# Joined VectorE operations over one buffer, first loads in smaller pieces, and a new order of emission, in a kernel that mixes a long convolution with a token MLP

## The chip, the cores and the metric

The kernel runs on one core of a Trainium2 chip. The core has several engines, each with its own instruction stream: TensorE (matmuls, "PE" in the profile), VectorE ("DVE"), ScalarE ("ACT"), GpSimd ("POOL"), and SyncE ("SP"), which here only issues DMAs. The engines wait for each other through semaphores. The metric is the device time of one execution in microseconds; lower is better.

## The reference, cut to what matters

```python
def reference(A_q, A_k, A_v, A_shift_k, A_ssm_k, A_ssm_D, B_x, B_w1, B_b1, B_w2, B_b2, gate_w):
    def _A_ref(q, k, v, shift_k, ssm_k, ssm_D):      # S = 2048, D = 640, 4 taps
        for t in range(ks):
            k_shift = k_shift + k_pad[:, t:t + S, :] * shift_k[:, ks - 1 - t][None, None, :]
        kv = k_shift * v
        kv_f = rfft2(kv_pad);  kf_f = rfft2(kf_pad)  # both padded to 2S = 4096
        y = irfft2(kv_f * kf_f)[:, :S, :]
        y = y + kv * ssm_D[None, None, :]
        return q * y
    def _B_ref(x, w1, b1, w2, b2):                   # F = 1536
        h = _layernorm(x, axis=-1)
        u = _gelu(jnp.einsum("bsd,sf->bdf", h, w1) + b1)
        return transpose(jnp.einsum("bdf,fs->bds", u, w2) + b2)
    x = A_q
    g = _sigmoid((x * gate_w).sum(-1, keepdims=True))
    return g * _A_ref(x, ...) + (1 - g) * _B_ref(x, ...)
```

All arrays are bf16. Branch A is a convolution along the 2048 tokens, done in the frequency domain, with one filter per channel; branch B is an MLP along the tokens. A gate per token mixes the two.

## The kernel before

**Tiling.** A tile has 128 partitions. Tokens are split by their residue modulo 8, so that a "slot" holds four residues of 640 channels each: 128 x 2560 elements (`SL = 4 * D`). X (the input q, which layer normalisation overwrites in place) has four slots X0 to X3; so have k and v.

**Stages.** (1) *W stage*: the filter `ssm` is loaded in two halves, transposed on TensorE (`transp`, five blocks of 128 channels for each half), copied from PSUM to `wT` on ScalarE or VectorE, and multiplied by the cosine and sine tables `FTB` (`fwd` for odd residues, `fwd_even` for the even ones). ScalarE evicts every result from PSUM to the spectra: C0 for the first half, C1 for the second. VectorE combines them (`mixing`). `fwd` makes groups of four matmuls per eviction, `fwd_even` groups of two. (2) *kv stage*: a load of k (`kn`) is copied to another layout (`kp`, `k_turn`), transposed by a DMA into `KT` (two for each half), and multiplied by a matrix of taps `KF` that GpSimd builds; ScalarE evicts it to `ksh`, VectorE multiplies by v (`kv`). (3) *A transforms*: kv is transformed with the same tables into C2 (first half) and C3 (second half) and mixed. (4) *w1*: twelve tiles of F, each a sum of 32 products of `ring` (pieces of w1) with normalised X (four blocks of eight matmuls, one block for each X slot), gelu on ScalarE into GT. Between the tiles VectorE multiplies X by the gate weights into `gq`, and ScalarE sums the rows. (5) *Products* of the spectra on VectorE (`cross`, `product`), with some additions made by accumulating DMAs from GpSimd's queue. (6) *Inverse*: VectorE's `invmix` and TensorE's `inverse` with the tables `GTB`, twice (h = 0, 1); (7) *w2*, sixteen tiles of 24 matmuls, interleaved with the inverse; ScalarE evicts with the scale 1 - g and the bias `c2` = (1 - g) * b2 into O. The inverse's results go through `cgb` (scaled by g), are multiplied by q and added to O on VectorE. For the last tile the bias is added to `cgb` beforehand (line 573) and two last operations (line 619) take the matmul's result straight from PSUM to O.

**Buffers.** The spectra C0 to C3 and SS, and the temporary tm0 and tm1 of the products, are separate tensors, each with two or four slots; SS and tm0 follow C3 in memory. One vector operation takes one tensor as an operand, with a pattern of strides over it, so operations over slots of two tensors are separate instructions.

**Order.** The program is written as a list of operations (one entry for each vector operation, activation, DMA, or run of matmuls). `_ORDER`, at the end of the file, is the order in which they are emitted, made beforehand by a planner; each engine runs its instructions in that order. `_SLOTS` says which of the four PSUM tiles pp0 to pp3 each run of matmuls uses. A tracker looks at what each operation reads and writes and puts in the semaphore waits. So a change of the list's length changes every number in `_ORDER`. `TAKES` says which of ScalarE and VectorE does a copy of a filter tile (`wT..`), a normalisation (`ln0` to `ln15`, one for each of the 16 residue tiles of X) or a relayout of k (`kp..`). All loads are on SP's queue, in the order of emission. SP's issue of a DMA waits for the semaphores that the tracker puts ahead of it, and everything behind it on SP waits with it.

Because helpers emit the operations, the profile's lines are those of the helpers: L298 is every matmul, L559 every tensor-tensor operation (`tt`), L573 and L574 tensor-scalar operations, L603 every activation (`act`), L613 the copy of `wT` on VectorE, L619 the last two operations, L272 every plain DMA, L265 the DMA transposes, L267 the accumulating DMAs, L884 the statistics, L694 and L698 the relayout of k on VectorE and ScalarE.

```python
SSM0 = ((0, 2), (2, 5))
def tab_load(i):
    a, b = ((0, NF - 2048), (NF - 2048, NF))[i]
    dma(FTB[:, a:b], dr(ftab, a, [[NF, 128], [1, b - a]]), 256 * (b - a), tok=f"f{i}")
```

Of the kernel before, what the change touches and what calls it, by code (L numbers as in the profile page):

```python
# [440 lines left out]
def _build(nc, A_q, A_k, A_v, A_shift_k, A_ssm_k, A_ssm_D, B_x, B_w1, B_b1, B_w2, B_b2, gate_w, out):  # L441
# [10 lines left out]
    with ExitStack() as es:  # L452
# [26 lines left out]

        def base_of(h):  # L480
            return T.mem[h.name][1]

        def V(h, off, dims, p0=0, pn=128):
            row = T.mem[h.name][2]
            return bass.AP(tensor=h, offset=p0 * row + off, ap=[[row, pn]] + [list(d) for d in dims])
# [21 lines left out]
        INVE = (1,)  # L507
        FALL, GALL = len(EVEN) < 2, len(INVE) < 2
# [7 lines left out]
        C = [alloc(f"C{i}", [128, 4, 4, D], BF16) for i in range(4)]  # L516
        SS = alloc("SS", [128, 2, 4, D], BF16)
        E_base = cur[0]
# [5 lines left out]
        gq = [alloc(f"gq{i}", [128, 2, D], BF16, at=base_of(Drow) + 5120 + 2560 * i) for i in range(2)]  # L524
# [12 lines left out]
        tm = [alloc(f"tm{i}", [128, 2, 4, D], BF16, at=E_base + 2 * SL * 2 * i) for i in range(2)]  # L537
# [142 lines left out]
        def x_load(hk):  # L680
            dma(X[:, hk, :, :], row8(A_q, hk), 128 * 5120, tok=f"x{hk}", rate=400.0)
# [32 lines left out]
        SSM0 = ((0, 2), (2, 5))  # L714
        TAKES = {'wT00': 'DVE', 'wT01': 'ACT', 'wT02': 'ACT', 'wT03': 'ACT', 'wT04': 'ACT', 'ln0': 'DVE', 'ln1': 'DVE', 'ln2': 'DVE', 'ln3': 'DVE', 'ln4': 'DVE', 'ln5': 'DVE', 'ln6': 'DVE', 'ln7': 'DVE', 'ln8': 'ACT', 'ln9': 'ACT', 'ln10': 'ACT', 'ln11': 'DVE', 'ln12': 'ACT', 'ln13': 'ACT', 'ln14': 'DVE', 'ln15': 'ACT', 'kp0': 'DVE', 'kp1': 'DVE', 'wT10': 'ACT', 'wT11': 'DVE', 'wT12': 'ACT', 'wT13': 'ACT', 'wT14': 'ACT', 'kp2': 'DVE', 'kp3': 'ACT'}
        ORDER = "x0 s00 s02 x1 f0 f1 x2 x3 s10 s12 w00 w01 k0 k1 w02 w03 gw t0 t1 v0 v1 k2 k3 v2 v3 t2 t3 w10 w11 w12 w13 g w20 w21 w22 w23".split()
# [13 lines left out]
        def tab_load(i):  # L730
            a, b = ((0, NF - 2048), (NF - 2048, NF))[i]
            dma(FTB[:, a:b], dr(ftab, a, [[NF, 128], [1, b - a]]), 256 * (b - a), tok=f"f{i}")
# [11 lines left out]
        tab_load(0)  # L744
        tab_load(1)
# [144 lines left out]
        def ln_scale(a, b):  # L890
# [21 lines left out]
            o_.dur, o_.lock = 1.05, False  # L912
# [27 lines left out]
        for h in range(2):  # L940
# [8 lines left out]
            if h == 0:  # L949
# [40 lines left out]
                mixing(C[0], SS, 0, fine=True, prio=MIXP)  # L990
# [55 lines left out]
        def mixing_acc(R, Th, Ts):  # L1046
# [3 lines left out]
            def pr(h, s, rev=False):  # L1050
                return V(h, s * SL + (1280 if rev else 0), [[-1280 if rev else 1280, 2], [1, 1280]])
            for i in range(2):
                tt("DVE", sl(Th, Ts + i), sl(R, i), sl(R, 2 + i), ALU.subtract)
# [6 lines left out]
        PACC = ()  # L1060
        mixing_acc(C[2], C[1], 0) if 0 in PACC else mixing(C[2], C[1], 0)
# [8 lines left out]
        for ft in range(FT):  # L1070
# [14 lines left out]
            if ft == 0:  # L1085
                act(gq[1][:, 0, :], gwb[:, :], ACT.Copy, acc=gws[:, :], name="gws").after.add(g_)
            if ft in (1, 3, 5, 7):
                hk = ft // 2
                for a in range(2):
                    gb = gq[a]  # L1090
                    tt("DVE", gb[:, :, :], X[:, hk, 2 * a:2 * a + 2, :], V(gwb, 0, [[0, 2], [1, D]]), ALU.mult)
                    for b in range(2):
                        t = 4 * hk + 2 * a + b
                        act(gb[:, b, :], gb[:, b, :], ACT.Copy, acc=gacc[:, t:t + 1], name="gsum")
# [52 lines left out]
        npr = [0]  # L1147

# [28 lines left out]
        def half(hs, i, rev=False):  # L1177
            h, s = hs
            if rev:
                return V(h, (s + i) * SL + 1280, [[-1280, 2], [1, 1280]])  # L1180
            return V(h, (s + i) * SL, [[1280, 2], [1, 1280]])

        def comp(hs, i, c):
            h, s = hs
# [194 lines left out]
```

## Time and profile before

| what | value |
|---|---|
| time, median of 3 runs | 181.4 us (181.2, 181.4, 181.61) |
| time of the profiled execution | 181.52 us |
| its span, first to last instruction | 179.7 us |
| mean granted clock of TensorE | 0.997 |
| TensorE's last matmuls of w2 | from 172.48 us, for 3.42 us |
| last two operations on VectorE (L619) | from 175.82 us, for 1.00 us |
| vector operations of L559 on 128x2560 and on 128x5120 elements | about 1.48 us and 2.82 us each |
| eviction of a 128x640 result by ScalarE | 0.718 us each, one every 0.61 us when in a row |
| loads: SP's issue | 0.44 to 0.59 us each when the queue is free |

The span is that of the profiled execution, and all positions in the text ("at 27.56 us") count from its start. The table of landings that the prediction uses comes from the trace's record of each DMA: a load issued by SP lands when the last of the 16 DMA engines has written its part. In the views, "idle before <-releaser" says how long an engine waited and for what; a group's "x8" is a run of eight like instructions, and overlapping matmuls make the shown time of a group longer than the time to the next group's start.

| load | landed at us | load | landed at us |
|---|---|---|---|
| ssm, first half, two pieces | 4.29, 6.82 | kn (first two) | 21.11, 24.36 |
| X0 | 8.40 | X2 | 22.72 |
| FTB, first piece | 9.98 | first w1 piece | 25.73 |
| X1, X3 | 11.78, 13.35 | KT, first pair | 28.81, 31.31 |
| ssm, second half, two pieces | 15.38, 18.27 | last v piece that is ahead of the second KT pair | 46.11 |
| FTB, second piece | 19.53 | KT, second pair | 49.70, 52.66 |

### The profile page before, as it was taken

Reading aid. Unit: us, or ns where it says so; the run is one execution under the profiler, and the core shown is the slowest. Engines: PE = TensorE matmul, PEld = TensorE weight load, DVE = VectorE, ACT = ScalarE, POOL = GpSimd, SP = SyncE. Lnnn points to the kernel's source line nnn. Section 1 sums busy time; section 2 is a strip of 40 time slices with the busy share of each in tenths; the row PEclk is TensorE's granted clock in tenths of the full one; section 3 lists DMA queues with packets and bytes.
Section 4 is the critical chain, followed back from the end, with each engine's and each line's share of the span. In section 5 each row is a group of like instructions: output and inputs, shape, how many; then the busy total and the mean of one; then the engine's idle time right before and its main releaser. Section 6 shows DMA issues by size and latency. Waiting matters only on the chain.

```text
span 179.7 us, 3292 instructions
## 1 busy us (share of the span) xinstructions
PE 171.4 (95%) x1364; PEld 135.0 (75%) x1364; DVE 167.2 (93%) x195; ACT 111.4 (62%) x174; POOL 42.1 (23%) x40
## 2 busy tenths in 40 slices
PE   7998689999999999999999999999999999999991
PEld 2676436787678766767777788999999998888780
DVE  2499889989999999999999999999999999999993
ACT  3489799999999999895891231033041306555860
POOL 1059924410000305200035110220085000024300
PEclk9999999999999999999999999999999999999998
DMA  5999999999989999998968997489899998919896
GB/s 182 358 383 408 403 200 181 325 395 385 141 169 306 334 212 334 226 209 269 387 166 146 197 170 241 123 148 178 318 285 198 199 198 222 379 68 191 190 278 217
DMA packets 31659, 44.57 MB, mean 248 GB/s; under 512 B 11673, under 2 KB 21018, under 8 KB 31516
## 3 DMA queue, kind: packets, MB, share of 16 engines
q1 hardware_dynamic: 26384, 33.20, 57.4%
q0 software_dynamic: 5200, 11.14, 35.0%
q8 instruction: 11, 0.18, 0.4%
q14 instruction: 4, 0.03, 0.0%
q10 hardware_dynamic: 60, 0.01, 0.0%
HBM read 27.96 MB, written 2.62 MB: 170 GB/s over the span
## 4 chain that ended last, share of the span: by engine, by line
PE 78%; DMA 8%; DVE 5%; ACT 4%; SPq 2%; issue 1%; DVEq 0%
PE pp L298 78%; DMA FTB<-ftab 8%; ACT C L603 3%; SPq L272 2%; DVE cgb L559 2%; DVE O L559 1%; DVE C L559 1%; ACT wT L603 1%; ACT cgb L603 0%; DVE O L619 0%; DVEq L412 0%; DVE cgb L573 0%; DVE q_hi L559 0%
## 5 line engine op out<-in xcount | busy, mean ns | idle before, releaser
L559 DVE TENSOR_TENSOR C<-C 128x2560 bf16<-128x2560 bf16 (+2 forms) x41 | 58.2, 1451 | 1.1 <-ACT C L603 1.0
L298 PE MATMUL pp<-X,ring 128*128 128x320 bf16 x384 | 56.9, 299 | 0.1
L298 PE MATMUL pp<-GT,W 128*128 128x320 bf16 x384 | 54.7, 300 | 0.0
L298 PEld LDWEIGHTS pp<-GT,W 128*128 128x128 bf16 x384 | 51.9, 144 | 1.3 <-ACT O L603 0.5
L298 PEld LDWEIGHTS pp<-X,ring 128*128 128x128 bf16 x384 | 37.3, 98 | 14.6 <-issue 0.5
L603 ACT ACTIVATE C<-pp 128x640 bf16<-128x640 f32 x64 | 41.3, 718 | 3.6 <-PE pp L298 3.4
L603 ACT ACTIVATE O<-pp,c,omg 128x640 bf16<-128x640 f32 x15 | 12.9, 882 | 29.8 <-PE pp L298 29.8
L298 PE MATMUL pp<-wT,FTB 128*128 128x320 bf16 x112 | 17.6, 300 | 1.9 <-ACT wT L603 0.7
L267 POOL DMA_DIRECT2D C<-C x8 | 10.9, 1915 | 26.7 <-DVE C L559 26.7
L603 ACT ACTIVATE GT<-pp,cc 128x640 bf16<-128x640 f32 x12 | 9.6, 797 | 11.9 <-PE pp L298 11.9
L603 ACT ACTIVATE cgb<-pp,gg 128x640 bf16<-128x640 f32 x16 | 12.2, 792 | 7.2 <-PE pp L298 7.0
L298 PEld LDWEIGHTS pp<-wT,FTB 128*128 128x128 bf16 x112 | 9.8, 97 | 8.3 <-ACT C L603 3.0
L559 DVE TENSOR_TENSOR tm<-C,C 128x2560 bf16<-128x2560 bf16 (+1 forms) x7 | 14.4, 2057 | 0.0
L267 POOL DMA_DIRECT2D C<-q_hi x6 | 5.9, 984 | 35.9 <-DVE q_hi L559 20.4
L884 DVE BATCH_NORM_STATS2 stats<-X 128x6 f32<-128x320 bf16 x32 | 13.4, 474 | 0.8 <-DMA X<-in_A_q_dram 0.7
L298 PE MATMUL pp<-C,GTB 128*128 128x320 bf16 x80 | 12.5, 299 | 0.0
L603 ACT ACTIVATE gq<-gq 128x640 bf16<-128x640 bf16 x16 | 11.7, 737 | 0.0
L559 DVE TENSOR_TENSOR SS<-C 128x2560 bf16<-128x2560 bf16 x8 | 11.7, 1478 | 0.0
L267 POOL DMA_DIRECT2D O<-q_hi x4 | 4.8, 1200 | 26.9 <-DVE q_hi L559 26.9
L559 DVE TENSOR_TENSOR C<-tm 128x2560 bf16<-128x2560 bf16 (+1 forms) x9 | 10.6, 1191 | 0.1
L559 POOL TENSOR_TENSOR KF<-cw,m 128x1120 bf16<-128x1120 bf16 x4 | 8.1, 2059 | 9.9 <-ACT cw L603 9.9
L603 ACT ACTIVATE ksh<-pp 128x1024 bf16<-128x1024 f32 (+1 forms) x12 | 10.2, 892 | 0.1
(72 smaller groups left out, 186.2 us busy)
## 6 DMA issues: line engine op xcount, KB each, us to landing
ring<-in_B_w_dram SPq DMA_DIRECT2D x12, 512.0 KB, 7.2
W<-in_B_w_dram SPq DMA_DIRECT2D x12, 512.0 KB, 4.7
C<-C POOLq DMA_DIRECT2D x8, 640.0 KB, 9.9
X<-in_A_q_dram SPq DMA_DIRECT2D x4, 640.0 KB, 9.5
kn<-in_A_k_dram SPq DMA_DIRECT2D x4, 640.0 KB, 12.5
out_dram<-O SPq DMA_DIRECT2D x7, 320.0 KB, 3.6
C<-SS POOLq DMA_DIRECT2D x3, 640.0 KB, 7.7
ssm<-in_A_ssm_k_dram SPq DMA_DIRECT2D x2, 768.0 KB, 8.6
```

What stands on the lines that cost most here:

```text
L267: ins = engobj.dma_start(out_ap, in_ap, accum_op=ALU.add, max_dma_last_dim=2560)
L272: ins = engobj.dma_start(out_ap, in_ap)
L298: ins = self.nc.tensor.matmul(ps_ap, lhsT=lhsT, rhs=rhs, start=start, stop=stop, skip_group_check=True)
L559: o_ = SC.add(eng, d, lambda s: T.op(eng, lambda e: e.tensor_tensor(o, a, b, op), rd, [o]), rd, [o], prio=prio, name="tt")
L603: return T.op("ACT", lambda e: e.activation(o, src, func, **kw), rr + [src], ww)
L884: ops.append(SC.add("DVE", 0.38, (lambda o, i: lambda s: T.op("DVE", lambda e: e.bn_stats(o, i), [i], [o]))(o, i), [i], [o]))
```

## The change

It has five parts.

1. The buffers SS, C0 to C3, tm0 and tm1 become windows (class `Win`) of one tensor AR of 22 slots. Operations that were the same on two tensors, or on neighbouring slots, become one: the two products with a late part (`product2` in place of two `product`), `cross` (one set of operations for each g in place of two, with the accumulating DMAs twice as large and half as many), the first operations of `invmix`, the first of `mixing_acc`, and the multiplications for the gate (`gq`, now one buffer of four tiles).
2. First loads: X0 comes in two parts, the first half of ssm in three instead of two, FTB in three instead of two; their order changes.
3. `TAKES`: the normalisations 9, 10 and 15 go from ScalarE to VectorE; of the filter tiles, wT00 and wT11 go from VectorE to ScalarE and wT04 and wT12 the other way.
4. In the last tile the bias is added by ScalarE (Identity with bias) instead of VectorE.
5. A new `_ORDER` and `_SLOTS`. Among other things, 32 matmuls of w1 (four blocks) lie between the transforms of the W stage (8 before), 80 ahead of the first A transform (72 before), and the run of w2 behind the last inverse has 20 matmuls (24 before). SP issues three w1 pieces ahead of the first pair of k's transposes (one before), and the load of `gwb` between the two transposes of the second pair. GpSimd's computation of 1/sqrt(variance) keeps its place in the order.

```diff
+        class Win:
+            def __init__(self, h, s0):
+                self.h, self.s0 = h, s0
+            def __getitem__(self, ix):
+                a = ix[1]
+                a = a + self.s0 if isinstance(a, int) else slice((a.start or 0) + self.s0, a.stop + self.s0)
+                return self.h[(ix[0], a) + tuple(ix[2:])]
...
-        C = [alloc(f"C{i}", [128, 4, 4, D], BF16) for i in range(4)]
-        SS = alloc("SS", [128, 2, 4, D], BF16)
+        AR = alloc("AR", [128, 22, 4, D], BF16)
+        SS, C, tm = Win(AR, 0), [Win(AR, 2 + 4 * i) for i in range(4)], [Win(AR, 18), Win(AR, 20)]
...
         def x_load(hk):
-            dma(X[:, hk, :, :], row8(A_q, hk), 128 * 5120, tok=f"x{hk}", rate=400.0)
+            n_ = 2 if hk in XH else 1
+            for i in range(n_):
+                w = 4 // n_
+                o0 = (1024 * (hk // 2) + 4 * (hk % 2) + w * i) * D
+                dma(X[:, hk, w * i:w * i + w, :], dr(A_q, o0, [[8 * D, 128], [1, w * D]]), 128 * 1280 * w, ...)
...
-        SSM0 = ((0, 2), (2, 5))
+        SSM0 = ((0, 1), (1, 3), (3, 5))
+        XH = (0,)
+        FTP = (0, 1024, NF - 2048, NF)
...
-            a, b = ((0, NF - 2048), (NF - 2048, NF))[i]
+            a, b = FTP[i:i + 2]
...
-            o_.dur, o_.lock = 1.05, False
+            o_.dur = 1.05
...
+            tt("DVE", sl(Th, Ts, 2), sl(R, 0, 2), sl(R, 2, 2), ALU.subtract)
             for i in range(2):
-                tt("DVE", sl(Th, Ts + i), sl(R, i), sl(R, 2 + i), ALU.subtract)
...
-                for a in range(2):
-                    gb = gq[a]
-                    tt("DVE", gb[:, :, :], X[:, hk, 2 * a:2 * a + 2, :], V(gwb, 0, [[0, 2], [1, D]]), ALU.mult)
+                tt("DVE", gq[:, :, :], X[:, hk, :, :], V(gwb, 0, [[0, 4], [1, D]]), ALU.mult)
...
+        def product2(a, v, into):
...
+            tt("DVE", late, Hg(a, 1), Hg(v, 0), ALU.mult)
+            for n_, g in enumerate((1, 0)):
+                dma(H(into[g], 1), V(q_hi, 2560 * n_, [[1280, 2], [1, 1280]]), 128 * 5120, stream="POOL", prio=0, accum=True)
+            tt("DVE", Pg(tg), Pg(a), Pg(v), ALU.mult)
+            tt("DVE", Hg(a, 1), Hg(a, 0), Hg(v, 1), ALU.mult)
+            tt("DVE", Hg(a, 0), Hg(tg, 0), Hg(tg, 1), ALU.subtract)
...
+            tt("DVE", V(AR, s0 * SL, [[SL, 2], [1, SL]]), y0, y1, ALU.add)
+            tt("DVE", y0, y0, y1, ALU.subtract)
...
-                    ts("DVE", cg[:, 1, :], cg[:, 1, :], c2[:, t:t + 1], None, ALU.add, mode=2)
+                    act(cg[:, 1, :], cg[:, 1, :], ACT.Identity, bias=c2[:, t:t + 1], name="c2")
...
-        chained(product, A1[1], A1[1], V0[1], tmp_of(q_hi, 0), V1[1])
-        chained(product, A1[0], A1[0], V0[0], tmp_of(q_hi, 1), V1[0])
+            chained(product2, A1, V0, V1)
```

## The prediction, made before the changed kernel was run

> **What bounds the kernel now.** I read the summary page first, then the chain of waits, then TensorE's timeline at the start, then the SP queue, and last the groups with shapes kept apart.
>
> ```profile
> span 179.7 us, 3292 instructions
> PE 171.4 (95%) x1364; PEld 135.0 (75%) x1364; DVE 167.2 (93%) x195; ACT 111.4 (62%) x174; POOL 42.1 (23%) x40
> ...
> PE   7998689999999999999999999999999999999991
> ...
> DVE  2499889989999999999999999999999999999993
> ...
> DMA  5999999999989999998968997489899998919896
> ```
>
> Each digit is a fortieth of the span, 4.5 us. Two engines look full. The chain says which of them ends last:
>
> ```profile
> PE 78%; DMA 8%; DVE 5%; ACT 4%; SPq 2%; issue 1%; DVEq 0%
> ```
>
> TensorE holds 78% of it, and in order of time the chain has PE from 26.87 to 165.6 us almost unbroken. The list of TensorE's waits from 30 to 176 us is empty, so a busy VectorE costs nothing there as long as it stays ahead. From one start to the next a 128x320 matmul takes 0.136 us (624 matmuls in the 85.58 us from 80.0: 0.137). By that pace TensorE loses 4.9 us between 30 and 176 us, in bits of 0.1 to 0.3, but some 9 us ahead of 30:
>
> ```profile
> 18.31 0.72 PE L298 MATMUL pp<-ident,ssm 128*128 128x128 bf16 x8 [1.23 <-DMA ssm<-in_A_ssm_k_dram]
> 19.58 0.72 PE L298 MATMUL pp<-wT,FTB 128*128 128x320 bf16 x4 [0.55 <-DMA FTB<-ftab]
> ...
> 22.01 2.88 PE L298 MATMUL pp<-wT,FTB 128*128 128x320 bf16 x18 [0.68 <-ACT wT L603]
> 25.04 0.45 PE L298 MATMUL pp<-wT,FTB 128*128 128x320 bf16 x2 [0.15 <-ACT C L603]
> 25.68 0.45 PE L298 MATMUL pp<-wT,FTB 128*128 128x320 bf16 x2 [0.20 <-ACT C L603]
> 26.28 0.45 PE L298 MATMUL pp<-wT,FTB 128*128 128x320 bf16 x2 [0.15 <-ACT C L603]
> 26.87 0.72 PE L298 MATMUL pp<-wT,FTB 128*128 128x320 bf16 x4 [0.15 <-ACT C L603]
> 27.56 1.25 PE L298 MATMUL pp<-X,ring 128*128 128x320 bf16 x8
> ```
>
> The brackets give the idle time before a group and its releaser. Two loads are late (1.23 and 0.55 us). Then comes the transform of the filter ("W stage"): pairs of matmuls that need 0.27 us of TensorE wait for an eviction that ScalarE repeats every 0.61 us. Measured start to start against the pace, the gaps from 20 to 28 us are 0.85, 0.20, 0.32, 0.36, 0.32, 0.32 and 0.13, in sum 2.5 us: 1.05 ahead of 25 us, 1.45 behind it. Only one block of eight w1 matmuls (27.56) lies between them as filling.
>
> **The change part by part.** The sum is made against the profiled execution, 181.52 us with a span of 179.7, so 1.8 us lie around the span; the median of the runs is 181.4.
>
> *Merged VectorE operations.* Counted in the two programs, 110 large additions and multiplications become 89 over the same number of elements.
>
> ```profile
> L559 DVE TENSOR_TENSOR C<-C 128x2560 bf16<-128x2560 bf16 x27 | 39.2, 1483 | 0.4 <-ACT C L603 0.4
> ...
> L559 DVE TENSOR_TENSOR C<-C 128x5120 bf16<-128x5120 bf16 x4 | 11.3, 2819 | 0.0
> ```
>
> Joining two saves between 0.069 us (from start-to-start times of 1.40 and 2.74) and 2 x 1.483 - 2.819 = 0.147 us. So 21 fewer save 1.45 to 3.1 us of VectorE. That work lies beside TensorE, which waits for it nowhere behind 30 us: worth 0, and without that cover 1.45. Cross products join two accumulating DMAs of 320 KB into one of 640 KB twice; the accumulations of 640 KB land 3.1 to 3.4 us apart now and stay beside other work: 0.
>
> *Normalisations moved.* Tiles 9, 10 and 15 leave ScalarE (0.952 us each by L603 X<-X,nm,rstd) for VectorE (0.36 start to start): -2.9 and +1.1 us. They run from 37.7 to 44.9; the table by windows has ScalarE busy 10.00 and VectorE 9.17 of the 10 us from 36 to 46, so this relieves the fuller one. Two transposed filter tiles go each way between the two (1.06 against 1.22 us): 0. All of it is cover for the next step.
>
> *First loads in pieces.* X0 goes in two parts, the first half of ssm in three, the table FTB in three, and one X load goes back. I summed the bytes in the new order of issue along the landing curve of now (X0 landed at 8.40, first FTB piece 9.98, ssm's second half 15.38 and 18.27, last FTB piece 19.53, X2 22.72, the first w1 piece 25.73). New: the first X half at 3.5, the FTB pieces at 11.0, 11.8 and 19.5, ssm's second half again 15.4 and 18.3, since the bytes ahead of it are the same, X2 at 21.1 and w1 at 24.0 and 25.4. VectorE starts earlier, but the two waits at 18.31 and 19.58 stay as they are, and TensorE has done the same work by 20.1: 0. The queue keeps the DMA engines at 9 tenths, and pieces of 327,680 to 524,288 B could cost nothing or up to 0.5 us (three more issues of 0.44 to 0.59 us on SP, of which the queue hides most, to 1.5 if it hid none). I take 0, as the queue is full, and keep 0 to 1.5 for the range.
>
> The Trainium skill speaks against pieces: page "DMA: Bandwidth & Descriptors", section "Anatomy of one DMA — SWDGE (gpsimd) path", has about 2.0 us fixed for a DMA issued by GpSimd, plus its bytes over 436 GB/s. Paid in turn on SP's queue, three more loads would by an estimate from that page cost 6 us. What that would be by rows is the last rival.
>
> *New order, W stage.* Four w1 blocks (32 matmuls, 4.36 us) now lie between the transforms instead of one. The first needs X0 normalised, which I place at 24.7 by VectorE's sum (0.405 us each for the statistics, 0.36 for a normalisation), so it starts at about 25.2. What is lost ahead of that stays (1.05 us: there is nothing else to run); of the 1.45 behind it I leave 0.15, since eight pairs lack 8 x (0.61 - 0.27) = 2.7 us and 4.36 us of other work stands there. **-1.3 us**; bounds 0 (X1, normalised at 27.65 for a use at 27.9, or w1 late) to -2.5 (all gaps filled).
>
> *New order, kv stage.* The gaps at 41.7, 47.9 and 56.6 are 0.28, 0.18 and 0.10; with eight more w1 matmuls ahead of the first A transform (80 against 72) I keep 0.2 of 0.56: **-0.3 us**. The first product k*v comes from VectorE at 45.8 for a use at 46.9, the second at 48.6 for 48.8, the pair behind them at 65.5 for 64.9 to 65.5. So TensorE's lead meets VectorE here, and 0 to 0.9 us may be given back; I take 0 and keep 0.9.
>
> *Transposes of k.* SP runs the four issues in order:
>
> ```profile
> 22.60 7.23 SPq L265 DMA_TRANSPOSE KT<-kp  x2
> ...
> 41.27 9.54 SPq L265 DMA_TRANSPOSE KT<-kp  x2
> 50.86 0.58 SPq L272 DMA_DIRECT2D gwb<-in_gate_w_dram  x1
> ```
>
> The second pair landed at 49.70 and 52.66; TensorE used it at 54.45, 1.8 us later. The first of that pair held SP for 6.36 us while v pieces were still landing (to 46.11), the others 3.1 to 3.7. Now three w1 pieces instead of one go ahead of the first pair, the third copy of k is ready at about 43.0, and the gwb load stands between the two issues. With 3.6 us for the first the second is issued at 47.2 and lands 5.0 later (the median to landing), 52.2, for a use at 52.1 to 52.4: 0 now, but no slack left. If it is late, kv blocks of the second half wait, behind them ksh's evictions on ScalarE, kv on VectorE and the second A transform.
>
> *Last addition.* 0.386 us (L573) leaves VectorE, and 0.737 to 0.952 comes on ScalarE, beside a VectorE addition of 0.485. The last w2 run behind the last inverse is 20 matmuls (24 now), 2.72 us, against two evictions, a product of 0.83, the addition on ScalarE and two final ones of 0.5: the end comes 0.95 us behind TensorE instead of 0.83. **+0.1**; bounds -0.2 to +0.3.
>
> Sum: 181.52 - 1.3 - 0.3 + 0.1 = **180.0 us**.
>
> **The rivals.**
> *Gaps only move* (181.4). For it: X1 has 0.25 us to spare, and the pair at 65.5 none. Against it: ScalarE and VectorE both have less to do there. The W stage gains 1.3, then 0.9 at kv and 0.4 for the pieces are given back: 181.5 at most, 181.4 with the kv stage's part. 12%.
> *The transposes become the wait* (slower, 182.6). If the first issue of the second pair holds SP for 6.36 us again, the second goes out at 43.0 + 6.4 + 0.5 (gwb) = 49.9 and lands 5.0 later at 54.9, 2.6 us behind its use at 52.3: 180.0 + 2.6 = 182.6. It decides from a landing at 53.7, where it has eaten the gain against the median (1.4). For it: the one earlier sample of this issue took that long, and the queue is fuller. Against it: v's last piece then should have landed when it starts, and three of four issues took 3.1 to 3.7. 20%.
> *All gaps go* (178.6): -2.5 and -0.56, with the tail's +0.1. For it: there are four blocks of filling. Against it: X0 isn't normalised before 24.7. 10%.
> *Each piece pays its latency* (185.6). The first load (524,288 B) lands 3.56 us after its issue, the second (786,432 B) 2.53 us behind it; at the second's pace 1.69 us of the first are transfer and 1.87 are latency. Three more loads ahead of the last FTB piece, each with that much unhidden, put it and the W stage 5.6 us later. Against it: with the queue full, loads of 655,360 B land 1.57 to 2.1 us apart, all of it transfer at the pace of 0.31 to 0.42 MB/us. 3%.
>
> **How the numbers follow.** Forecast 180.0 with 55% (its own range 179.3 to 180.9), the others as given. Against the median of 181.4, 0.2% or 0.36 us is what a measurement can tell from no change. Faster: 55 + 10, 0.65. Same: the 12 of the gaps that move, 0.12. Slower: 20 + 3, 0.23. The range reaches from 178.6 (all gaps go) to 182.6 (the transposes), and leaves out the pieces' latency and transposes later still.
>
> **What would show it.** Right: several groups "pp<-X,ring" x8 between 25 and 32 us with no bracket of over 0.1; the last FTB piece still at 19.5; about 1.5 us less between 20 us and the first A transform; VectorE 1 to 2 us less busy and PE waits still empty behind 30 us; the last KT landing ahead of 52.4. Wrong: a bracket "<-DMA KT" or "<-DVE kv" between 50 and 66 us, "<-ACT X" or "<-DMA ring" near 27 us, FTB or ssm landing later than 19.8, or a chain whose last pieces hold more ScalarE than the final addition.

## The result, and the profile after

The changed kernel takes 182.3 us in the median of 15 runs (181.51 to 183.38), the kernel before 181.4 us (180.89 to 181.92) on the same chip: a ratio of 1.0056, 95% interval 1.0039 to 1.0074. It is slower by 0.56%, about 1.0 us, where 1.4 us less were forecast. The profiled execution is the longest of the 15, 183.38 us with a span of 181.5; a second profile of the same kernel, `after_again`, is used beside it. All ratios and intervals here leave out executions more than 1.5% above the fastest of the same kernel, which the medians and ranges in microseconds include; this matters for `after_tail3`, `t3_w2` and `t3_w2_old` alone.

The page of the changed kernel, parts 1, 2 and 4:

```profile
span 181.5 us, 3269 instructions
PE 171.1 (94%) x1364; PEld 134.7 (74%) x1364; DVE 167.3 (92%) x176; ACT 110.5 (61%) x172; POOL 37.3 (21%) x38
...
PE   7889689999999999999999999999999999999970
...
PE 79%; DMA 11%; ACT 3%; SPq 3%; issue 1%; DVE 0%; DVEq 0%
```

TensorE does the same work, but its last digit is a 0 and not a 1, so the span goes on for longer after TensorE has ended. VectorE runs 19 instructions fewer for the same busy time. To see where the 1.8 us between the spans of the two profiled executions lie, I took for each matmul the time to the next one's start, less its pace (0.133 us for 320 columns, and in proportion), and summed what is left over by the time of start:

| us that TensorE loses beyond its pace | before | changed |
|---|---|---|
| 0 to 20 us (loads, first half of the W stage) | 6.44 | 7.33 |
| 20 to 30 us (second half of the W stage) | 2.77 | 1.97 |
| 30 to 70 us (kv stage, first A transforms) | 1.92 | 1.94 |
| 70 to 110 us | 0.94 | 0.76 |
| 110 to 130 us (w2 begins) | 0.50 | 1.01 |
| 130 us to the last matmul | 1.30 | 0.97 |
| last matmul starts at | 175.60 | 175.69 |
| from there to the end of the span | 4.11 | 5.83 |

Up to TensorE's last matmul the kernels are level (175.60 and 175.69). All but 0.1 us of the difference lies behind it, where only the last operations and the stores of the output run. In four other profiles with the changed order of the end (`after_again`, `after_joined`, `after_c2_dve` and `after_x1late`, below) that stretch is 5.3 to 5.7 us.

TensorE's timeline of the changed kernel at the start (start, duration, operation, idle before and its releaser):

```profile
12.40 4.52 PE L298 MATMUL pp<-wT,FTB 128*128 128x320 bf16 x32 [0.64 <-DMA FTB<-ftab]
16.76 1.13 PE L298 MATMUL pp<-ident,ssm 128*128 128x128 bf16 x16
19.53 1.69 PE L298 MATMUL pp<-ident,ssm 128*128 128x128 bf16 x24 [1.64 <-DMA ssm<-in_A_ssm_k_dram]
21.05 3.51 PE L298 MATMUL pp<-wT,FTB 128*128 128x320 bf16 x22
24.72 0.45 PE L298 MATMUL pp<-wT,FTB 128*128 128x320 bf16 x2 [0.15 <-ACT AR L621]
25.31 1.09 PE L298 MATMUL pp<-wT,FTB 128*128 128x320 bf16 x6 [0.15 <-ACT AR L621]
26.64 1.25 PE L298 MATMUL pp<-X,ring 128*128 128x320 bf16 x8 [0.24 <-ACT AR L621]
27.72 1.71 PE L298 MATMUL pp<-wT,FTB 128*128 128x320 bf16 x10
29.27 1.25 PE L298 MATMUL pp<-X,ring 128*128 128x320 bf16 x8
```

The w1 blocks do what was foreseen: behind the start of the first one, at 26.64, there is no bracket. But it starts at 26.64 and not at 25.2, and the waits ahead of it stay (0.15, 0.15 and 0.24, as the view counts them). X is not the reason: VectorE's fourth normalisation ended at 24.44, near the 24.7 that I had. The block stands behind the pairs in TensorE's order. Both loads at the start are later than before.

The end of VectorE's timeline, first before and then in the changed kernel:

```profile
158.74 0.81 DVE L559 TENSOR_TENSOR q_hi<-cgb,q_hi 128x1280 bf16<-128x1280 bf16 x1
159.47 1.48 DVE L559 TENSOR_TENSOR C<-SS 128x2560 bf16<-128x2560 bf16 x1
160.87 0.82 DVE L559 TENSOR_TENSOR q_hi<-cgb,q_hi 128x1280 bf16<-128x1280 bf16 x1
161.61 2.88 DVE L559 TENSOR_TENSOR SS<-C 128x2560 bf16<-128x2560 bf16 x2
164.41 0.82 DVE L559 TENSOR_TENSOR q_hi<-cgb,q_hi 128x1280 bf16<-128x1280 bf16 x1
```

```profile
157.38 0.82 DVE L577 TENSOR_TENSOR q_hi<-cgb,q_hi 128x1280 bf16<-128x1280 bf16 x1
158.12 5.81 DVE L577 TENSOR_TENSOR AR<-AR 128x2560 bf16<-128x2560 bf16 x4
163.85 1.55 DVE L577 TENSOR_TENSOR q_hi<-cgb,q_hi 128x1280 bf16<-128x1280 bf16 x2
```

Four products of q with the inverse's result are added to O by GpSimd's accumulating DMAs, and an output can be stored only when its accumulation has landed. Before, the second product came at 160.87, ahead of the last two of four `invmix` operations. Now four `invmix` operations run in a row, and the second and third products follow together at 163.85. GpSimd's timeline, before and changed:

```profile
159.85 1.20 POOL L267 DMA_DIRECT2D O<-q_hi  x1 [22.75 <-DVE q_hi L559]
161.99 1.20 POOL L267 DMA_DIRECT2D O<-q_hi  x1 [0.94 <-DVE q_hi L559]
165.53 1.20 POOL L267 DMA_DIRECT2D O<-q_hi  x1 [2.34 <-DVE q_hi L559]
167.57 1.20 POOL L267 DMA_DIRECT2D O<-q_hi  x1 [0.84 <-DVE q_hi L559]
```

```profile
158.50 1.20 POOL L267 DMA_DIRECT2D O<-q_hi  x1 [20.31 <-DVE q_hi L577]
164.97 2.43 POOL L267 DMA_DIRECT2D O<-q_hi  x2 [5.26 <-DVE q_hi L577]
167.91 1.20 POOL L267 DMA_DIRECT2D O<-q_hi  x1 [0.51 <-DVE q_hi L577]
```

The second accumulation is issued 3.0 us later. On SP's queue the stores stand in order behind it; the timeline of SP from 168 us, before and changed:

```profile
171.09 6.10 SPq L272 DMA_DIRECT2D out_dram<-O  x7
```

```profile
169.56 8.07 SPq L272 DMA_DIRECT2D out_dram<-O  x8
```

Before, two of the nine stores were issued by 166.1; now one is, and eight are issued from 169.56 on, within 8.07 us. From the records of the DMAs, they then land one behind the other, about 0.9 us apart for most stores of 327,680 B:

```
issued and landed, before:   164.0 166.99 | 166.1 170.70 | 171.1 173.74 | ... | 175.9 178.48 | 176.8 179.42
issued and landed, changed:  162.6 165.28 | 169.6 174.35 | 171.3 175.13 | ... | 175.9 179.15 | 177.1 181.23
```

The last store is issued 0.2 us later than before and lands 1.8 us later. A store counts as landed when the last of its 16 parts has, one for each DMA engine, and the last parts show two delays. Of the last 16 parts to land, 12 were there 3.0 us behind the last matmul's start before, and 3.8 us in the changed kernel: that is the row of stores. The very last came 3.8 and 5.5 us behind it, so one engine ends 0.8 us after these 12 before, and 1.7 us in the changed kernel. There its packets go on at 179.15, when a transfer of 16,384 B on the instruction queue, 0.92 us long from 178.24, has just ended, and from 179.4 they are the only ones; the link between the two is read from their times alone. `after_again`, where such a transfer came at 173.6, has 3.7 and 5.0 us.

The chain of waits of the changed kernel, in order of time, shows nothing of this:

```profile
171.91 4.09 PE pp L298 x30
176.00 0.04 issue
176.04 0.55 DVE O L637
176.59 0.46 DVEq L412
```

It follows instructions and ends at 177.05, while the span runs to 181.5 with the stores' transfers. A chain that ends 4.5 us ahead of the span (2.9 before) says that something which is no instruction ends last.

### The profile page after: what moved, and what is told of

Read it like the earlier page. It is cut to its first block, busy times and chain, and to the rows that moved or that the text cites. A ratio compares the mean times of both kernels' runs of the same rounds, so it can differ in the third digit from the quotient of the medians.

```text
span 181.5 us, 3269 instructions
## 1 busy us (share of the span) xinstructions
PE 171.1 (94%) x1364; PEld 134.7 (74%) x1364; DVE 167.3 (92%) x176; ACT 110.5 (61%) x172; POOL 37.3 (21%) x38
## 4 chain that ended last, share of the span: by engine, by line
PE 79%; DMA 11%; ACT 3%; SPq 3%; issue 1%; DVE 0%; DVEq 0%
PE pp L298 79%; DMA ssm<-in_A_ssm_k_dram 7%; DMA W<-in_B_w_dram 4%; SPq L272 3%; ACT AR L621 2%; ACT wT L621 1%; DVE O L637 0%; DVEq L412 0%; SPq L199 0%
## 5 line engine op out<-in xcount | busy, mean ns | idle before, releaser
L577 DVE TENSOR_TENSOR AR<-AR 128x2560 bf16<-128x2560 bf16 (+3 forms) x67 | 116.1, 1764 | 1.2 <-ACT AR L621 0.6
L298 PE MATMUL pp<-X,ring 128*128 128x320 bf16 x384 | 56.3, 299 | 0.2 <-ACT AR L621 0.2
L621 ACT ACTIVATE AR<-pp 128x640 bf16<-128x640 f32 x64 | 40.5, 719 | 5.1 <-PE pp L298 4.8
L267 POOL DMA_DIRECT2D AR<-AR x11 | 13.6, 1802 | 75.6 <-DVE AR L577 53.2
L298 PE MATMUL pp<-AR,GTB 128*128 128x320 bf16 x112 | 16.6, 299 | 0.0
L298 PEld LDWEIGHTS pp<-AR,GTB 128*128 128x128 bf16 x112 | 10.7, 98 | 4.3 <-ACT O L621 0.4
L621 ACT ACTIVATE wT<-pp 128x1024 bf16<-128x1024 f32 x8 | 7.9, 1048 | 4.3 <-PE pp L298 4.3
L267 POOL DMA_DIRECT2D AR<-q_hi x4 | 5.8, 1580 | 15.3 <-DVE q_hi L577 9.4
L298 PE MATMUL pp<-KF,KT 128*128 128x128 bf16 (+1 forms) x160 | 8.8, 213 | 0.0
```

The source lines that it names most:

```text
L267: ins = engobj.dma_start(out_ap, in_ap, accum_op=ALU.add, max_dma_last_dim=2560)
L298: ins = self.nc.tensor.matmul(ps_ap, lhsT=lhsT, rhs=rhs, start=start, stop=stop, skip_group_check=True)
L577: o_ = SC.add(eng, d, lambda s: T.op(eng, lambda e: e.tensor_tensor(o, a, b, op), rd, [o]), rd, [o], prio=prio, name="tt")
L621: return T.op("ACT", lambda e: e.activation(o, src, func, **kw), rr + [src], ww)
```

## The experiments

Each run was compared with the kernel before on the same chip, whose median was 181.3 to 181.5 us. Numbers in the diffs are places in the list of operations; a line names an engine's order.

**1. The changed kernel again, and parts of it (first chip).** `after_again` changes nothing.

> The changed kernel once more. In its first profile TensorE's last matmul starts 0.08 us later than before, and the span ends 5.8 us behind it instead of 4.1; the last output lands at 181.2 us. Theory 'tail' (the outputs pile up at the end: eight of nine issued in the last 8 us): the distance from the last matmul to the end is 5 us or more here too, and ssm's last piece may lie anywhere. Theory 'start' (more pieces make the loads late: ssm's second half landed at 19.48 us, before at 18.27): it lands at 19.2 or later again, and the tail is nearer to 4.5. Both can hold; the time 0.4 to 0.8% above before.

Measured: 182.63 us, ratio 1.0075 (1.0045 to 1.0105). Its profile has the last matmul at 174.9 and 5.3 us behind it, so TensorE ended 0.7 us earlier than before and the time was still longer. ssm's last part landed at 18.27 here, as before, so the 19.48 of the first profile is not in every execution.

`before_pieces` puts only the smaller loads into the kernel before:

```diff
-        SSM0 = ((0, 2), (2, 5))
+        SSM0 = ((0, 1), (1, 3), (3, 5))
-            a, b = ((0, NF - 2048), (NF - 2048, NF))[i]
+            a, b = (0, 1024, NF - 2048, NF)[i:i + 2]
-            dma(X[:, hk, :, :], row8(A_q, hk), ...)
+            for i in range(2 if hk == 0 else 1): dma(X[:, hk, ...], ...)
```

> The kernel before with only the splitting of the first loads (X0 in two, the first half of ssm in three, FTB in three, in the old order of bytes). Theory 'start': three more loads make some DMA engines lag, ssm's second half lands at 19.0 to 19.5 us and the kernel is 0.7 to 1.2 us slower than before. Rival (splitting is free, the lag in the changed kernel has another cause): it lands at 18.0 to 18.5 and the time is within 0.3 us of before.

Measured: 181.85 us, 1.0028 (1.0015 to 1.0041). The pieces cost 0.5 us by the ratio, less than the theory had and more than the rival, where the prediction had taken 0. The first W transform starts at 11.98 instead of 10.94, ssm's last part lands at 18.64 instead of 18.27 and FTB's at 19.91 instead of 19.53. Not all of this is the pieces: `before_late_q`, below, has the old loads, and its first W transform starts at 11.69.

`after_joined` joins two pieces of ssm and two of FTB again in the changed kernel (X0 stays in two, and the filter copies stay where they were):

```diff
-        SSM0 = ((0, 1), (1, 3), (3, 5))
-        FTP = (0, 1024, NF - 2048, NF)
+        SSM0 = ((0, 3), (3, 5))
+        FTP = (0, NF - 2048, NF)
```

> The changed kernel with two loads fewer ahead of W: the ssm blocks 0 to 2 in one load, FTB's first 2048 columns in one. Theory 'start': ssm's second half lands 0.5 to 1 us earlier than in the changed kernel, and the time falls by as much. Rival: no difference over 0.3 us against the changed kernel in this batch.

Measured: 182.57 us, 1.0062 (1.0049 to 1.0076): nothing came back, though ssm landed at 17.91. This left the pieces open until the last runs.

`after_qhi` moves one late product of q ahead of `invmix`'s last two operations, its accumulation with it:

```diff
 VectorE:
+  641 (q_hi *= cgb0),
   649, 648 (invmix),
-  641 (q_hi *= cgb0),
   627 (q_hi *= cgb1)
```

> The changed kernel with one vector operation moved: the product of q with the inverse's residue 3 of the first half runs at about 161 us instead of 163.9, ahead of the last two operations of 128x2560 in invmix, and its accumulating DMA with it. Theory 'tail': the second output is issued some 2.5 us earlier (167 instead of 169.6), fewer outputs are queued at the end, and the kernel is 0.4 to 1 us faster than the changed one. Rival: the end is set by the last product and its own output, so nothing changes, or TensorE stalls 0.3 us for the delayed invmix and it is 0.3 us slower.

Measured: 182.63 us, 1.0063 (1.0049 to 1.0076), no gain. The stretch behind the last matmul falls to 3.5 us, but that matmul starts 1.1 us later, at 176.82. The product still waited for its eviction on ScalarE and ran at 163.18 only; `invmix` behind it was late, and TensorE stood for 1.28 us at 164.1. The move needs the eviction as well.

**2. The end of the kernel, both ways (second chip).** `after_tail2` moves the eviction too, and puts two w2 runs where TensorE would stand:

```diff
 ScalarE:
+  638 (evict cgb0),
   626 (evict cgb1), 633,
-  638 (evict cgb0),
 VectorE:
+  641 (q_hi *= cgb0),
   649, 648 (invmix),
-  641 (q_hi *= cgb0),
 TensorE:
+  546, 547 (w2),
   670, 668, 656 (inverse),
-  546, 547 (w2),
```

> The changed kernel with the outputs of the first half brought forward: the eviction and the product of residue 3 ahead of invmix' last two operations (about 161.7 us), and two w2 runs of four matmuls ahead of the transform that waits for these, so that TensorE has no stall of 1.28 us as in after_qhi. Theory 'tail': the last matmul stays at 175.0 to 175.7 us, the distance to the end falls from 5.3-5.8 to 3.6-4.4, and the time from 182.6 to 181.2 (180.9 to 181.7). Rival (the end is not set by when the first half's outputs start): it stays at 182.3 to 182.8.

Measured: 181.6 us, 1.0014 (0.9992 to 1.0035), 0.7 us less than the changed kernel and no longer to be told from the kernel before. GpSimd's timeline has the second accumulation at 162.26 (164.97 in the changed kernel):

```profile
162.26 1.20 POOL L267 DMA_DIRECT2D O<-q_hi  x1 [2.34 <-DVE q_hi L577]
```

The second store is issued at 167.2 (169.6), and the stretch behind the last matmul is 3.5 us; the last of the 16 parts comes only 0.05 us behind the twelfth. The last matmul is not where it was expected, at 175.0 to 175.7, but at 176.85: TensorE still stood for 0.66 us at 168.4, and it lost 0.2 us more than in the changed kernel's profile both in the first 30 us and between 110 and 130 us.

`before_late_q` does the opposite: it takes the kernel before and puts one product of q where the changed kernel has it.

```diff
 VectorE:
-  645 (q_hi *= cgb1),
   668, 669 (invmix),
+  645 (q_hi *= cgb1),
   659 (q_hi *= cgb0)
```

> The kernel before with one vector operation and its accumulating DMA moved the other way: the product of residue 2 runs behind invmix' last two operations (at 163.7 instead of 160.9 us), as in the changed kernel. Theory 'tail': last matmul unchanged (175.4 to 175.9), distance to the end 5.0 to 5.8 instead of 4.1, time 0.8 to 1.4 us over before. Rival: within 0.3 us of before.

Measured: 182.55 us, 1.0059 (1.0047 to 1.0071): this one move costs 1.1 us, as much as the whole change. GpSimd's and SP's timelines of this run have the pattern of the changed kernel:

```profile
159.63 1.20 POOL L267 DMA_DIRECT2D O<-q_hi  x1 [22.75 <-DVE q_hi L559]
164.69 2.43 POOL L267 DMA_DIRECT2D O<-q_hi  x2 [3.86 <-DVE q_hi L559]
```

```profile
168.85 8.66 SPq L272 DMA_DIRECT2D out_dram<-O  x8
```

TensorE's last matmul starts at 175.38 (175.60 before), and 5.4 us follow it instead of 4.1. The last store is even issued 0.2 us earlier than before (176.66 and 176.85), and lands 1.0 us later (180.46 and 179.42).

`after_c2_dve` gives the last addition back to VectorE:

```diff
-  act(cg[:, 1, :], cg[:, 1, :], ACT.Identity, bias=c2[:, t:t + 1], name="c2")
+  ts("DVE", cg[:, 1, :], cg[:, 1, :], c2[:, t:t + 1], None, ALU.add, mode=2)
```

> The changed kernel with the last addition back on VectorE. Theory 'tail' (outputs queue up): 182.4 to 182.8 as the changed kernel, since only the last of nine outputs is touched. Rival (ScalarE's addition lengthens the last chain): 0.3 us or more faster.

Measured: 182.2 us, 1.0046 (1.0029 to 1.0063). Against the changed kernel's 1.0056 that is no difference these runs can tell; the addition is not where the loss is.

`after_x1late` issues the load of X1 behind the last piece of FTB, so that ssm and FTB land earlier:

```diff
 SP:
-  6 (X1),
   FTB, FTB, X3, ssm, ssm, FTB,
+  6 (X1),
   7 (X2)
```

> The changed kernel with the load of X1 behind the last piece of FTB, so 655,360 B fewer ahead of ssm's second half. Theory 'start' (TensorE waits there for these bytes): ssm's second half lands 1.3 to 1.8 us earlier, at 16.6 to 17.8, TensorE's wait at 17.7 us goes and the last matmul comes 0.5 to 1.5 us earlier; with the tail as it is (outputs queue) the time falls by 0 to 1 us. Rival: X1's statistics, 4.5 us later, delay VectorE and the w1 blocks, and TensorE loses as much between 25 and 50 us as it gained: no change or slower.

Measured: 187.87 us, 1.0363 (1.0333 to 1.0393). The loads did land earlier (ssm 16.04, FTB 17.31), but a filter copy stands on VectorE behind X1's statistics, and TensorE waited for it. TensorE's timeline, and the table by windows (length; busy time of PE, PEld, DVE, ACT and POOL; granted clock; DMA share; GB/s):

```profile
19.64 1.54 PE L298 MATMUL pp<-wT,FTB 128*128 128x320 bf16 x8 [0.29 <-ACT wT L621]
26.09 4.38 PE L298 MATMUL pp<-wT,FTB 128*128 128x320 bf16 x20 [4.91 <-DVE mv L911]
```

```profile
21.00:26.00 5.00, 0.18 (x2) 0.00 (x0) 5.00 (x20) 1.52 (x3) 1.39 (x2) 0.98 1.07 371
26.00:28.50 2.50, 2.41 (x10) 1.37 (x11) 2.50 (x8) 1.32 (x2) 1.27 (x2) 0.50 0.33 108
28.50:31.00 2.50, 2.25 (x14) 1.14 (x12) 2.50 (x11) 1.83 (x4) 0.26 (x1) 0.86 0.01 3
```

The idle time costs twice: 4.91 us of waiting, and then matmuls at a granted clock of 0.50, from 25.77 to 29.18 us by the trace's record of the clock.

**3. The W stage (third chip).** `after_tail3` is `after_tail2` with a third w2 run moved, and the base for the rest:

```diff
 TensorE:
+  548 (w2),
   654 (inverse),
-  548 (w2),
```

> after_tail2 with one more w2 run of four matmuls placed where TensorE still stalled 0.66 us (168.4). Theory 'tail': last matmul 0.3 to 0.7 us earlier than in after_tail2, distance to the end 3.4 to 4, the time 181.0 to 181.6. If the end were set by the queue of outputs alone, this changes nothing (181.6).

Measured: 181.35 us, 0.9993 (0.9974 to 1.0011). With the end mended, the change costs nothing that these runs can tell.

`after_t3_x1` adds the late X1, with X1's statistics and a relayout of k behind the filter copy on VectorE:

```diff
 SP:
-  6 (X1),
   FTB, FTB, X3, ssm, ssm, FTB,
+  6 (X1),
   7 (X2)
 VectorE:
+  183 (wT12),
   statistics of X1,
-  183 (wT12),
```

> after_tail3 with X1's load behind FTB's last piece, and this time X1's statistics on VectorE behind the copy of the filter tile that TensorE waited 5.1 us for in after_x1late. Theory 'start' (bytes ahead of ssm's second half cost TensorE time one for one): that half lands at 16 to 17 us, TensorE does not wait there, the W stage ends 1 us or more earlier, and if VectorE keeps up the time is 180.0 to 180.8. Rival (VectorE, idle for X1 from about 15 to 18 us, is late afterwards): waits on X or on products of k and v appear behind 26 us and the time is 181 to 183.

Measured: 182.41 us, 1.0057 (1.0038 to 1.0077). ssm lands at 16.40 and FTB at 18.36, earlier than in any other run but `after_x1late`, and TensorE gains nothing: from start to start it loses 0.26, 0.47, 0.29 and 0.36 us at the filter copies instead, then 0.57 at X.

`after_t3_m1` puts the first w1 block ahead of the pairs that have gaps, with other PSUM tiles, and loads the first w1 piece ahead of the first piece of k (that move on SP is not in the cut):

```diff
 TensorE:
+  377 (w1, X0),
   202 (W pair), ...
-  377 (w1, X0),
```

> after_tail3 with the first w1 block of eight matmuls ahead of the pairs of the W stage that wait for evictions, in a PSUM tile that is free then, and the first w1 piece loaded ahead of the first k piece. Theory 'order' (in all profiles of the changed kernel the three gaps of 0.15, 0.32 and 0.32 us lie ahead of the first w1 block, and 0.40 just before it): these 1.2 us shrink to 0.5 or less, the W stage ends 0.5 to 0.8 us earlier, the time is 0.3 to 0.8 below after_tail3. Rival (ScalarE's evictions bound the stage wherever the block lies): the gaps move behind the block, no change within 0.2 us.

Measured: 181.78 us, 1.0023 (1.0004 to 1.0042). The gaps move behind the block (0.31, 0.32 and 0.32 us at 27.1 to 28.3, 0.47 at 32.2). The reason stands in ScalarE's timeline of `after_again`:

```profile
21.16 6.88 ACT L621 ACTIVATE AR<-pp 128x640 bf16<-128x640 f32 x11
```

and in that of the kernel before:

```profile
21.84 7.37 ACT L603 ACTIVATE C<-pp 128x640 bf16<-128x640 f32 x12
```

One eviction every 0.60 to 0.62 us from start to start, with no break, in both orders. Other work between the pairs fills TensorE's time, but the pairs can't end earlier than their evictions.

**4. A load of w2 (fourth chip).** Near 114 us most profiles of the changed order show a wait that the kernel before does not have; here TensorE's timeline of the changed kernel:

```profile
109.84 4.51 PE L298 MATMUL pp<-GT,W 128*128 128x320 bf16 x32
114.55 5.66 PE L298 MATMUL pp<-GT,W 128*128 128x320 bf16 x40 [0.20 <-DMA W<-in_B_w_dram]
```

Start to start, 0.37 us are lost there, and 0.24 to 0.66 in the others; `after_joined` and `pair_tail3` show none. `t3_w2` moves one load of w2, whose issue waits long on SP, behind three others that need not wait:

```diff
 SP:
-  516 (w2, second half),
   457, 458, 459 (w2, first half),
+  516 (w2, second half),
```

> after_tail3 with one load moved on SP's queue: the first w2 piece of the second half (into a part of ring0 that the last w1 matmuls still read until about 107 us) goes behind the last pieces of the first half, which stood behind it on the queue. Theory 'w2' (the wait of 0.4 to 0.6 us on W at 113 to 115 us in the profiles of the changed kernel comes from that place on the queue): the wait goes, and the time falls by 0.3 to 0.5 us against after_tail3, to about 180.9. Rival (the pieces are late because the accumulating DMAs share the engines): the wait stays and so does the time.

Measured: 186.34 us in the median (183.32 to 187.84, the widest range of all runs here), ratio 1.0186 (1.0141 to 1.0231). The wait near 114 us is gone, but most of the loads now go out between 90 and 107 us, at the same time as GpSimd's accumulations into AR, and these land late: the one issued at 94.69 at 108.22 (in `after_tail2` issued at 95.11 and landed at 106.42). VectorE's timeline of `after_tail2`, then VectorE's and TensorE's of `t3_w2` and its table by windows (a profiled execution of 186.93 us, so the sizes are those of a long one):

```profile
110.74 2.83 DVE L577 TENSOR_TENSOR q_hi<-AR 128x5120 bf16<-128x5120 bf16 x1 [0.47 <-DMA AR<-q_hi]
```

```profile
112.43 2.83 DVE L577 TENSOR_TENSOR q_hi<-AR 128x5120 bf16<-128x5120 bf16 x1 [2.60 <-DMA AR<-q_hi]
...
120.57 0.17 DVE L577 TENSOR_TENSOR c<-omg,cc 128x16 f32<-128x16 f32 x1
```

```profile
121.71 2.62 PE L298 MATMUL pp<-GT,W 128*128 128x320 bf16 x9 [2.18 <-ACT O L621]
```

```profile
119.00:121.70 2.70, 0.53 (x4) 0.24 (x2) 2.70 (x3) 0.93 (x2) 0.00 (x0) 0.98 1.10 193
121.70:125.00 3.30, 3.29 (x13) 2.12 (x14) 3.30 (x3) 1.62 (x2) 0.00 (x0) 0.50 0.77 139
```

The bias c for ScalarE's evictions into O is computed on VectorE behind that product, at 120.57 instead of 118.89; w2's evictions wait for it and TensorE for a PSUM tile. As far as the profiles of `t3_w2` and `t3_w2_old` show, the load that blocked SP's queue had kept this traffic apart.

`t3_w2_old` takes the first loads back to those of before as well, with the order of the start and the PSUM tiles that go with them.

```diff
 SP:       order of t3_w2
-        SSM0 = ((0, 1), (1, 3), (3, 5))
-        XH = (0,)
-        FTP = (0, 1024, NF - 2048, NF)
+        SSM0 = ((0, 2), (2, 5))
+        XH = ()
+        FTP = (0, NF - 2048, NF)
-        TAKES = {'wT00': 'ACT', ..., 'wT04': 'DVE', ...}
+        TAKES = {'wT00': 'DVE', ..., 'wT04': 'ACT', ...}
```

> t3_w2 with the first loads whole again (X0 in one, the first half of ssm in two, FTB in two, in the order of the kernel before) and the transposes, evictions and first vector operations in the order that suits them. Theory 'start' (the pieces cost 0.4 to 0.5 us, as in before_pieces): TensorE's first transform starts at 11 instead of 12 to 13 us, ssm's second half lands at 18.0 to 18.4, the time is 0.3 to 0.7 us below t3_w2 and varies less. Rival (the pieces buy VectorE an earlier start that is needed): waits on X or on products of k and v, 0.3 us or more slower than t3_w2.

Measured: 184.5 us, 1.0114 (1.0068 to 1.016): the stall at 118 us stays (2.99 us). By the ratios it is 1.3 us faster than `t3_w2`, but the two intervals overlap, so this is a hint, and no more, that the first loads count in the changed kernel.

**5. The first loads (fifth and sixth chip).** `t3_old` has the same start and the mended end of `after_tail3`, with SP's order for w2 as in the changed kernel.

> The changed kernel with the four moves of after_tail3 (ACT's eviction of the inverse's second residue, its product with q and its accumulating DMA ahead; three w2 runs ahead of two transforms) and with the first loads as they were before (ssm's first half in two pieces, X0 whole, FTB in two; the first copy of wT on VectorE, the fifth on ScalarE). SP's order behind the loads is unchanged. Theory (the split loads cost about 0.5 us, as before_pieces showed): the first matmuls of the W stage start near 11.7 instead of 12.4, ssm's last piece lands by 18.3, and the time is 180.8, ratio 0.995 to 0.998, faster than before. Rival (ScalarE bounds the W stage and takes back whatever the start gains, as in after_t3_x1 and after_t3_m1): the first A transform starts no earlier than in after_tail2, time 181.3, ratio 0.998 to 1.001.

Measured: 181.07 us, 0.998 (0.9954 to 1.0006). The first A transform starts at 47.42 (48.85 and 47.97 in the two profiles of the changed kernel), which speaks for the theory; the time alone does not decide. So the kernels of `after_tail3` and `t3_old` were run side by side on one chip, as `pair_tail3` (with the pieces) and `pair_old` (without):

> The kernel of after_tail3, run beside that of t3_old on one chip, to compare the two starts directly. Both theories: about as before, 181.2 to 181.5, ratio 0.998 to 1.001.

> The kernel of t3_old (first loads and the filter copies taken back as well). Theory (the split loads cost the changed kernel about 0.5 us or more, and t3_old's first A transform at 47.4 instead of 49.1 reaches the end): 0.5 to 1.0 us below pair_tail3 in the median, ratio to before 0.993 to 0.997. Rival (the earlier start is given back behind the first A transform, by the load of w2 or by VectorE): within 0.25 us of pair_tail3.

Measured: `pair_tail3` 181.66 us, 1.0005 (0.9981 to 1.0029); `pair_old` 180.93 us, 0.9961 (0.9938 to 0.9983). By the medians, the pieces and the filter copies and order that go with them cost 0.7 us; the two intervals just touch. TensorE's timeline of `pair_tail3` and of `pair_old`:

```profile
12.53 4.52 PE L298 MATMUL pp<-wT,FTB 128*128 128x320 bf16 x32 [0.70 <-DMA FTB<-ftab]
...
18.88 1.68 PE L298 MATMUL pp<-ident,ssm 128*128 128x128 bf16 x24 [0.86 <-DMA ssm<-in_A_ssm_k_dram]
```

```profile
11.09 4.51 PE L298 MATMUL pp<-wT,FTB 128*128 128x320 bf16 x32
16.79 2.93 PE L298 MATMUL pp<-ident,ssm 128*128 128x128 bf16 x40 [1.19 <-DMA ssm<-in_A_ssm_k_dram]
```

Without pieces the first transform does not wait for FTB and starts 1.4 us earlier. The first A transform then starts 0.5 us earlier (47.89 and 48.41), and in these two profiles the end of TensorE's work shows none of it: the last matmul starts at 175.64 and 175.53, as `pair_old` has the wait near 114 us (0.66 us) and `pair_tail3` does not. So the 0.7 us rests on the times alone. This version is the best of the study: 0.4% faster than the kernel before in the pair, though in `t3_old`, the same kernel, the interval still included no change.

## Why the prediction was wrong, by its own steps

- **Last addition, +0.1: the step that failed.** It took the end of the kernel to be the chain of operations behind TensorE. That chain came out as priced: the last operation ends 1.36 us behind the last matmul's start, 1.22 before. But the new order also moved a product of q past two `invmix` operations on VectorE, and the prediction did not follow it to its accumulating DMA and to the stores behind that on SP's queue. Its price is +1.1 us put in alone (`before_late_q`), and 0.7 to 1.1 us come back when it is mended (`after_tail2`, and `after_tail3` by the ratios 1.0056 and 0.9993).
- **First loads, 0 with bounds to 1.5.** Mis-sized: +0.5 us alone (`before_pieces`), about 0.7 us in the changed kernel with the end mended, there together with the filter copies and the order of the start. I summed bytes along the landing curve; in the changed kernel's first profile FTB's first piece landed at 12.35 where I had 11.0, and in most profiles with these loads ssm's last part landed between 18.3 and 19.6 where I had 18.3. That `after_joined` gave nothing back says that joining two of the three tensors is not enough; which of X0, the copies or the order it is was not tried. The price that I worked out from the Trainium skill, page "DMA: Bandwidth & Descriptors", section "Anatomy of one DMA — SWDGE (gpsimd) path", 6 us for three more loads paid in turn, does not hold on SP's queue here: 0.5 to 0.7 us were measured.
- **New order, W stage, -1.3.** The mechanism was right and the size too large: 0.5 to 0.8 us less loss from 20 to 30 us in five profiles of the changed order, and none in `after_joined` and `after_tail2` (2.8 us, as before), where TensorE waits for filter copies instead (0.29 and 0.20 us, as the view counts them). In the changed kernel's first profile the blocks fill what lies behind 26.6, but the pairs ahead of the first block still lose about 1.2 us, start to start (0.15, 0.32, 0.32 and 0.40). The bound is ScalarE's evictions, and bringing the block ahead gained nothing (`after_t3_m1`).
- **kv stage, -0.3.** Not found: 1.92 and 1.94 us lost between 30 and 70 us. No wait for kv came either, so nothing was given back there. The 4.9 us that the prediction has TensorE lose between 30 and 176 us belong to a pace of 0.133 us, with which the table above is made (4.7 us); by the 0.136 that it names they would be 1.9. No term of the sum rests on it.
- **Transposes of k, 0, with a rival at 182.6.** The time came out near that rival's, but its mechanism did not occur. The first transpose of the second pair held SP for 3.65 us, not 6.36. The last KT did land at 53.72, where the prediction had the rival decide, but TensorE's use of it came at 54.50 and not at 52.3, so there is no wait for KT.
- **Merged operations, 0.** VectorE is not seen to hold up the time, so this 0 stands. The durations of the tensor-tensor operations fell from 149.14 to 146.02 us, 0.15 for each of 21, but operations in a row overlap, and the time in which one of them runs fell only from 142.12 to 141.38, 0.035 for each where I had 0.069 at least. With the normalisations that came in, VectorE is as busy as before, so my sign "1 to 2 us less busy" was wrong.
- **Not in the sum: the load of w2** near 114 us, 0.26 to 0.66 us where it is seen. No kernel took it away by itself, so its worth in time was not measured.

Together: with start and end mended, the version is 0.7 us faster than before in `pair_old` and 0.4 in `t3_old`; the end's 1.1 us and the start's 0.7 turn that into the 1.0 us of loss. How much of the 0.4 to 0.7 us is the new order of the W stage is open, as the mended end is itself shorter than that of before: 3.4 us behind the last matmul against 4.1, with that matmul at 175.64 (`pair_old`) and 174.77 (`t3_old`) against 175.60. Whether the kernel before would gain from the same end was not tried. Two costs that the prediction had at 0.1 and 0 took more than what was gained.

## What to carry to other kernels

Follow every operation that a new order moves to its last DMA, and that DMA to the queue in which the stores wait; where the chain of waits ends several us ahead of the span, look at the stores: here they set the end, and when the second one left mattered more than when the last did. Other work between transforms pays only until the engine that evicts them is full. A DMA that blocks its queue may be what keeps later loads from colliding with earlier traffic, so a wait taken away there needs a look at what will now run at the same time.

## What the runs showed of the hardware

- **The clock after an idle TensorE.** After 4.91 us without work the granted clock was 0.50 from 25.77 to 29.18 us (`after_x1late`); after 2.18 us it was 0.50 from 121.62 to 125.03 (`t3_w2`), 3.41 us both times. After the 1.64 us of the changed kernel's wait for ssm it stayed at 1.00. The Trainium skill, page "TensorE: Matmul & The Clock Gate", section "Part 1: The HAM clock gate (the "warmup" mystery)", has half rate after an idle window of about 3.4 us and full rate after as long a busy one: the 3.41 us of ramp agree, but 2.18 us of idle were enough here. Half of 3.41 us is 1.7, so by an estimate that wait cost nearly its own length again.
- **One late DMA engine.** In every profile a transfer of 16,384 B on the instruction queue, of about 1.1 us, starts at 14.6 to 17.2 us, and in most of them one of the 16 parts of the loads lands late from then on: in the kernel before, 15 parts of ssm's last piece landed between 16.2 and 16.59 us and the last at 18.27. A load counts as landed with its last part, so this sets the wait for ssm. That the two belong together is read from their times alone; it was not tried.
- **Small first loads spread the engines.** In the changed kernel the first and the last of the 16 parts of a load lie 1.1 to 1.6 us apart from the second load on, before the transfer above begins (0.4 to 0.6 in the kernel before).
